# Sliding-window attention with a SwiGLU block: k and q of two chunks transposed by DMA, and the steps around them set in another order

## The chip, the cores and the metric

The kernel runs on one core of one Trainium2 chip. The metric is the device time of one execution in microseconds (us). TensorE is called PE, its weight load PEld, VectorE DVE, ScalarE ACT, GpSimd POOL and SyncE SP, as in the profile. POOL and SP issue most of the DMAs here: POOL the loads from HBM, which also turn float32 into bfloat16, SP the DMA transposes from SBUF to SBUF.

## The reference

Eight batches of eight heads, 576 positions, head dimension 64. Each position attends to itself and the 63 before it; the result, with the heads side by side as 512 features, goes through a SwiGLU block.

```python
scores = scale * np.matmul(q, k.transpose(0, 1, 3, 2))
rel = pos[:, None] - pos[None, :]
mask = (rel >= 0) & (rel < window)          # window = 64
attn = softmax(np.where(mask, scores, -1e9))
x = np.matmul(attn, v)                       # (8, 8, 576, 64) -> (4608, 512)
...
g = x @ w_gate                               # (512, 1536)
silu = g * (1.0 / (1.0 + np.exp(-g)))
val = x @ w_val                              # (512, 1536)
return (silu * val @ w_out).astype(np.float32)   # (1536, 512)
```

## The kernel before, in words

The 4608 rows are cut into 36 **chunks** of 128 rows, n = 0 to 35, and nine **groups** of four chunks (512 rows), c = 0 to 8. A chunk's attention needs its own keys and the 64 before.

What is done to a chunk, by the names in the code:

- *Loading.* `load(n, "kq")` (line 309) brings k and q of one chunk as 128 rows of eight heads of 64, one POOL DMA each (two when a batch ends inside the chunk). `load2(st)` (327) brings k or q of two chunks at once in another layout, eight rows of one head behind each other, 256 KB in one POOL DMA. The rings: eight buffers each of kn and qn, two buffers each for `load2`.
- *Transposing.* The scores need k and q with the head dimension on the partitions, in kT and qT. `T(n, x)` (362) does it with one DMA transpose on SP (recorded at line 370). `T64(st)` (373) does k and q of two chunks from the layout of `load2` with 64 transposes of 64x64 on PE (line 385) into two PSUM banks, from which four copies (line 255 on ACT or 256 on DVE) go to kT and qT.
- *Scores.* `S2(n)` (772) makes the scores of chunks n and n + 1 on PE (24 matmuls each, lines 471 and 475), four exponentials on ACT (483) and two products with the mask on DVE (497).
- *Attention times v.* `B2(n)` (787) is one block: scores of n + 2, the first half of attention times v of n and n + 1 (`AVpair`, line 729), scores of n + 3, the second half, then normalisation on DVE (760, 764) into xb, and the masks.
- *`X(n)`* (799) transposes xb into xT, the input of the feed-forward part; from chunk 6 on by a DMA transpose on SP (808).

And to a group: `F(c, fs, lo, hi)` (926) computes the hidden features fs (blocks of 128, f = 0 to 11) for the rows lo to hi of group c: gate and value matmuls on PE (918), tanh on ACT (899), two products on DVE (904, 906), result in hT. `O(c, u)` and `O2(c, u)` (937, 947) are the output of chunk u of group c, twelve matmuls (962), with the copy out of PSUM on ACT or DVE, and `store` writes it. `F` of half a group with two features is 16 matmuls, and `F` of a whole group with one feature 8.

The order of the work is written out by hand in `build` (1057), call by call up to the second group, then in a loop over the groups from c = 2. The loop begins at line 1195. Each engine has its own queue and takes its instructions in the order of the calls; waits on semaphores are derived from what each step reads and writes. PSUM banks, once `lru` is set, are taken in the order of longest unused. Three things are tied to a place in this order: loads with a gate (`self.lastF`) go out when the F before them has ended on PE, DMA transposes wait in SP's queue in the order of the calls, and POOL's queue likewise.

Around the change the order before is, on PE: AVw(6) and X(6), X(7); T64(4) with its copies on ACT; O(0,1); F(1) of features 6, 7 and 8, 9 on the first half; S2(8); T64(5) with its copies; F(1) of 10, 11 on the first half; F(1) of 0, 1 on the second half; O2(0,2); B2(8); F(1) of 2, 3 and of 4, 5; O2(0,3); B2(10); F(1) of 6, 7, of 8, 9 and of 10, 11; O(1,0), which has F(2) of feature 0 in its middle, behind its ninth matmul; F(2) of feature 1; O2(1,1); B2(12).

Of the kernel before, what the change touches and what calls it, by code (L numbers as in the profile page):

```python
# [153 lines left out]
class _Kernel:  # L154
# [644 lines left out]
    def X(self, n, eng="sp", kind="f"):  # L799
        if n >= NCH:  # L800
            return
        g = self.g
        ix, it, u = n % 4, (n // 4) % self.NX, n % 4
        xb = self.xb[ix]
        xo = self.xT[it][:, :, 128 * u:128 * u + 128]
        xk = [("xb", ix, 0), ("xb", ix, 1)]
        if eng == "sp":
            g.op("sp", lambda e: e.dma_start_transpose(xo, xb[:, :]), reads=xk, writes=[("xT", it, u)], dma=True)
            return
        self.Xp(n, kind)(eng)  # L810
# [115 lines left out]
    def F(self, c, fs, lo=0, hi=512, mid=None, side=False):  # L926
        do = self.Fp(c, fs, lo, hi, side)
        for a in range(len(fs)):
            do("Wg", a)
        if mid:  # L930
            mid()
        do("tan", 0)
        for a in range(len(fs)):
            do("Wv", a)
        do("end", 0)

    def O(self, c, u, mid=None):
        io = (4 * c + u) % self.NO
        self.Omm(c, u, 0, 512, "act", [("ost", io), ("osth", io)], mid=mid)
        self.store(c, u)  # L940
# [95 lines left out]
            self.load(n, "v")  # L1036

    def next_loads(self):
        self.load2(5)

    def after_loads(self):
        for n in (12, 13):
# [14 lines left out]
    def build(self):  # L1057
        F, S, AV, X, O = self.F, self.S, self.AV, self.X, self.O
# [64 lines left out]
        ev = self.T64(2)  # L1123
# [12 lines left out]
        ev = self.T64(3)  # L1136
# [14 lines left out]
        ev = self.T64(4)  # L1151
        for u in range(2):
            ev("k", u, "act")
            ev("q", u, "act")
        O(0, 1)
        F(1, (6, 7), 0, 256)
        self.after_loads()
        F(1, (8, 9), 0, 256)
        self.init_kmask()
        self.S2(8)  # L1160
        ev = self.T64(5)
        for u in range(2):
            ev("k", u, "act")
            ev("q", u, "act")
        for n in (12, 13):
            self.Tkq(n)
        F(1, (10, 11), 0, 256)
        F(1, (0, 1), 256, 512)
        self.O2(0, 2)
# [5 lines left out]
        for n in (14, 15):  # L1175
            self.load(n, "kq", self.lastF)
        F(1, (4, 5), 256, 512)
        self.O2(0, 3)
        self.B2(10)
        self.store(0, 3)  # L1180
        F(1, (6, 7), 256, 512)
        self.T(14, "k")
        X(10)
        X(11)
# [6 lines left out]
        for n in (16, 17, 18):  # L1191
            self.load(n, "kq")
        self.T(16, "q")
        O(1, 0, lambda: F(2, (0,)))
        for c in range(2, NFC):
            for u in range(4):
                n = 4 * c + u + 4
                if (c, u) != (2, 0):
                    F(c, (3 * u,))
                F(c, (3 * u + 1,))  # L1200
                if (c, u) == (3, 0):
                    self.loop_loads(n - 1)
                two = n < NCH and u % 2 == 0
                v = u + 1 if c == 2 else u
                if two:
                    self.O2(c - 1, v)
                elif v < 4 and (n < NCH or u < 3):
                    O(c - 1, v)
                if two:
                    self.B2(n)  # L1210
                    self.store(c - 1, v)
                    if u:
                        X(n)
                        X(n + 1)
                    for m in (n + 4, n + 5):
                        self.T(m, "k")
                    for m in (n + 5, n + 6):
                        self.T(m, "q")
                    if not u:
                        X(n)  # L1220
                        X(n + 1)
                F(c, (3 * u + 2,))
                if u % 2 and n <= NCH and (c, u) != (2, 3):
                    self.loop_loads(n)
                elif (c, u) == (2, 0):
                    for m in (14, 15):
                        self.load(m, "v", self.lastF)
                if n >= NCH and u == 3:
                    O(c - 1, u)
# [46 lines left out]
```

## Time and profile before

| | |
|---|---|
| median of three runs | 325.45 us (325.27 to 325.52) |
| the profiled execution's own time | 325.72 us |
| its span, first to last instruction | 324.0 us |
| PE busy | 314.4 us, 97% |
| DVE, ACT, POOL busy | 218.6, 125.6, 106.5 us |
| PE transposes of line 385 | 256 in the whole kernel, four times 64 |
| DMA transposes of line 370 (k, q) | 48, median 4.0 us to landing |
| DMA transposes of line 808 (xT) | 30, median 3.5 us to landing |

In a timeline row stand the start, the length, the engine, the line, the operation, what is written from what, and the count of merged instructions; behind it in brackets idle time of the engine and what ended it. A row of waits has the engine and line that waited, what it waited for, the total in us, how often, and the longest. A row of DMA issues ends with the median time from issue to landing. Matmuls are pipelined: a row's length holds the tail that the next row overlaps, so the time that work takes on PE is read from start to start.

### The profile page before, as it was taken

To read this page: it belongs to the slowest core of one execution; us is meant where nothing else is said; L and a number is where in the kernel's file an instruction comes from. 1 tells how busy PE (TensorE), PEld (TensorE's weight loads), DVE (VectorE), ACT (ScalarE), POOL (GpSimd) and SP (SyncE) were. 2 spreads that over 40 slices of the span, in tenths; PEclk is the share of its full clock that TensorE was granted. 3 is DMA by queue.
4 is the path that set the end of the run, shared out by engine and by line. 5 is a ranking of instruction groups with operands and counts; after the bars stand their busy time and mean duration, and the time that the engine had idled before them with its cause. 6 is when DMAs were issued, how large, how long until landed. Compare 5 with 4: busy or idle time off the path is not lost.

```text
span 324.0 us, 8018 instructions
## 1 busy us (share of the span) xinstructions
PE 314.4 (97%) x3411; PEld 169.3 (52%) x3446; DVE 218.6 (67%) x408; ACT 125.6 (39%) x226; POOL 106.5 (33%) x138
## 2 busy tenths in 40 slices
PE   7989999999999999999999999999999999999996
PEld 5655677777545454545454544545454544444444
DVE  6778985788576966766767585958586767555510
ACT  3825565643433442433333232424242422222311
POOL 6999711643626061507060607060402000000000
PEclk9999999999999999999999999999999999999999
DMA  7999999999999799959997998999677212000012
GB/s 189 177 197 187 201 184 176 104 169 142 166 155 152 124 109 137 165 103 133 129 120 118 146 139 83 148 133 159 73 110 96 69 34 65 34 32 32 34 65 97
DMA packets 148403, 39.59 MB, mean 122 GB/s; under 512 B 131344, under 2 KB 143376, under 8 KB 148368
## 3 DMA queue, kind: packets, MB, share of 16 engines
q0 software_dynamic: 100032, 18.36, 71.7%
q1 hardware_dynamic: 42864, 10.89, 23.5%
q10 hardware_dynamic: 5472, 9.83, 9.5%
q8 instruction: 27, 0.44, 0.6%
q14 instruction: 8, 0.07, 0.1%
HBM read 37.75 MB, written 9.44 MB: 146 GB/s over the span
## 4 chain that ended last, share of the span: by engine, by line
PE 91%; DMA 2%; POOL 2%; issue 1%; DVE 1%; ACT 1%; ACTq 0%
PE ps L918 56%; PE ps L962 29%; DMA Wv<-in_moe_w_val_dram 2%; PE ps L729 2%; PE ps L521 2%; POOL va L325 1%; PE ps L471 1%; PE ps L475 0%; ACT xT L255 0%; PE ps L385 0%; ACT sig L899 0%; POOL ks L335 0%; PE ps L552 0%; POOL qs L335 0%; POOL Wg L345 0%
## 5 line engine op out<-in xcount | busy, mean ns | idle before, releaser
L918 PE MATMUL ps<-xT,Wv 128*128 128x512 bf16 (+1 forms) x484 | 110.4, 351 | 1.6 <-DMA Wv<-in_moe_w_val_dram 0.9
L904 DVE SCALAR_TENSOR_TENSOR uu<-sig,ps 128x512 bf16<-128x512 bf16 x108 | 73.8, 683 | 56.2 <-ACT sig L899 55.9
L918 PE MATMUL ps<-xT,Wg 128*128 128x512 bf16 (+1 forms) x481 | 107.9, 351 | 2.3 <-issue 2.2
L899 ACT ACTIVATE sig<-ps 128x512 bf16<-128x512 f32 x108 | 64.9, 603 | 89.1 <-PE ps L918 89.1
L962 PE MATMUL ps<-Wo,hT 128*128 128x512 bf16 (+1 forms) x436 | 97.4, 373 | 0.5 <-DVE hT L906 0.2
L906 DVE SCALAR_TENSOR_TENSOR hT<-uu,ps 128x512 bf16<-128x512 bf16 x108 | 74.2, 687 | 4.7 <-PE ps L918 1.0
L918 PEld LDWEIGHTS ps<-xT,Wv 128*128 128x128 bf16 x496 | 48.4, 98 | 45.7 <-DMA Wv<-in_moe_w_val_dram 1.1
L918 PEld LDWEIGHTS ps<-xT,Wg 128*128 128x128 bf16 x496 | 46.8, 98 | 42.7 <-ACT xT L255 0.2
L962 PEld LDWEIGHTS ps<-Wo,hT 128*128 128x128 bf16 x444 | 43.3, 98 | 49.0
L325 POOL DMA_DIRECT2D kn<-in_k_dram x27 | 23.0, 855 | 112.0 <-PE ps L918 112.0
L325 POOL DMA_DIRECT2D va<-in_v_dram x40 | 34.2, 882 | 24.9 <-PE ps L918 24.9
L255 ACT ACTIVATE ost<-ps 128x512 f32<-128x512 f32 (+1 forms) x22 | 12.9, 588 | 53.2 <-PE ps L962 53.2
L531 ACT ACTIVATE pt<-ps 128x512 bf16<-128x512 f32 x36 | 18.6, 602 | 29.0 <-PE ps L521 29.0
L256 DVE COPY ost<-ps 128x512 f32<-128x512 f32 (+1 forms) x15 | 10.1, 673 | 29.2 <-PE ps L962 29.2
L325 POOL DMA_DIRECT2D qn<-in_q_dram x27 | 23.2, 865 | 0.0
L483 ACT ACTIVATE pt<-ps 128x512 bf16<-128x512 f32 x28 | 14.5, 602 | 13.8 <-PE ps L475 13.8
L764 DVE TENSOR_TENSOR xb<-ps,rc 128x512 bf16<-128x512 f32 (+2 forms) x39 | 18.8, 509 | 0.5
L729 PE MATMUL ps<-va,pt 64*64 64x65 bf16 x800 | 12.3, 192 | 0.0
L497 DVE TENSOR_TENSOR pt<-pt,kmask 128x1024 bf16<-128x1024 bf16 x18 | 11.5, 681 | 0.0
L729 PEld LDWEIGHTS ps<-va,pt 64*64 64x64 bf16 x800 | 10.4, 107 | 0.0
L497 DVE TENSOR_TENSOR pt<-pt,mask 128x1024 bf16<-128x1024 bf16 x14 | 9.3, 688 | 1.1 <-ACT pt L483 1.0
L760 DVE RECIPROCAL rc<-ps 128x8 f32<-128x8 f32 (+2 forms) x39 | 5.7, 173 | 6.3 <-PE ps L729 6.3
(76 smaller groups left out, 141.7 us busy)
## 6 DMA issues: line engine op xcount, KB each, us to landing
out_dram<-ost ACTq DMA_DIRECT2D x35, 256.0 KB, 3.3
va<-in_v_dram POOLq DMA_DIRECT2D x32, 128.0 KB, 5.3
kn<-in_k_dram POOLq DMA_DIRECT2D x21, 128.0 KB, 3.9
qn<-in_q_dram POOLq DMA_DIRECT2D x21, 128.0 KB, 4.7
Wg<-in_moe_w_gate_dram POOLq DMA_DIRECT2D x6, 256.0 KB, 7.2
Wv<-in_moe_w_val_dram POOLq DMA_DIRECT2D x6, 256.0 KB, 8.2
Wo<-in_moe_w_out_dram POOLq DMA_DIRECT2D x4, 384.0 KB, 13.6
ks<-in_k_dram POOLq DMA_DIRECT2D x3, 256.0 KB, 10.5
```

What stands on the lines that cost most here:

```text
L255: return self.g.op("act", lambda e: e.activation(d, a, ACTF.Copy), reads=reads, writes=writes, after=after)
L325: self.g.op("pool", lambda e, d=d, a=a: e.dma_start(d, a), writes=ks, dma=True, after=gate)
L483: g.op("act", lambda e, po=po, p=p: e.activation(po, sv[p], ACTF.Exp, scale=SCALE), reads=[bx[p][1]], writes=[pk[p]])
L497: self.g.op("dve", lambda e: e.tensor_tensor(pt, pt, m, ALU.mult), reads=pk + mk, writes=pk)
L531: g.op("act", lambda e, po=po, p=p: e.activation(po, sv[p], ACTF.Exp, scale=SCALE), reads=[bx[p][1]], writes=[pk[p]])
L729: x = e.matmul(o, ab[0], ab[1], start=first, stop=phase == 1, skip_group_check=True)
L764: g.op("dve", lambda e, av=av, hs=hs, w=w, rc=rc, xo=xo: e.tensor_tensor(xo[:, :, hs, :], av[:, :, :, 0:64], rc[:, :, hs].unsqueeze(3).to_ ...
L899: g.op("act", lambda e: e.activation(sig[:, 0:w], G[:, 0:w], ACTF.Tanh, scale=0.5), reads=[gk], writes=[("sig", i)])
L904: g.op("dve", lambda e: e.scalar_tensor_tensor(uu[:, 0:w], sig[:, 0:w], 1.0, G[:, 0:w], ALU.add, ALU.mult), reads=[("sig", i), gk], writes ...
L906: g.op("dve", lambda e: e.scalar_tensor_tensor(out, v3(uu), 0.5, v3(V), ALU.mult, ALU.mult), reads=[("uu", i), vk], writes=[("hT", ih, f, ...
L918: r = e.matmul(bank[:, a * n:a * n + n], W[:, kk, f * 128:f * 128 + 128], xT[:, kk, lo:hi], start=(kk == 0), stop=(kk == NK - 1))
L962: r = e.matmul(OB[:, 0:n], hT[:, f, 128 * u:128 * u + 128], self.Wo[:, f, lo:hi], start=(f == 0), stop=(f == NF - 1))
```

## The change

Chunks 10 and 11 no longer go through `load2` and T64(5): k and q of each are loaded singly (four POOL DMAs) and transposed by four DMA transposes on SP, which stand in SP's queue behind X(7) and ahead of those of chunks 12 and 13. S2(8) moves up by two F steps, behind O(0,1), and the F of 6, 7, 8, 9 follow it, so that the gate of the loads of 12, 13 (the F of 6, 7) lies behind S2(8). F(1) of 6, 7 on the second half goes ahead of O2(0,3) and B2(10). O(1,0) is no longer split; O(1,1) follows it, and then F(2) of feature 0. In the loop's first group O2(1,2) takes the place of O2(1,1), O2(1,3) stays, and O(1,2) is gone from between them; O(1,1) is copied out by ACT in place of DVE, O(1,2) by DVE in place of ACT.

```diff
     def next_loads(self):
-        self.load2(5)
+        for n in (10, 11):
+            self.load(n, "kq")
...
         O(0, 1)
+        self.init_kmask()
+        self.S2(8)
+        for n in (10, 11):
+            self.Tkq(n)
         F(1, (6, 7), 0, 256)
         self.after_loads()
-        F(1, (8, 9), 0, 256)
-        self.init_kmask()
-        self.S2(8)
-        ev = self.T64(5)
-        for u in range(2):
-            ev("k", u, "act")
-            ev("q", u, "act")
         for n in (12, 13):
             self.Tkq(n)
+        F(1, (8, 9), 0, 256)
         F(1, (10, 11), 0, 256)
...
         F(1, (4, 5), 256, 512)
+        F(1, (6, 7), 256, 512)
         self.O2(0, 3)
         self.B2(10)
         self.store(0, 3)
-        F(1, (6, 7), 256, 512)
...
-        O(1, 0, lambda: F(2, (0,)))
+        O(1, 0)
+        O(1, 1)
+        F(2, (0,))
...
-                v = u + 1 if c == 2 else u
+                v = (2, 4, 3, 4)[u] if c == 2 else u
```

## The prediction

> **What bounds the kernel now.** I read the page first: engine shares, clock, the chain that ended last. The list of what TensorE (PE) waited for came next, over 49 to 324 us, all that follows the edits.
>
> ```profile
> span 324.0 us, 8018 instructions
> PE 314.4 (97%) x3411; PEld 169.3 (52%) x3446; DVE 218.6 (67%) x408; ACT 125.6 (39%) x226; POOL 106.5 (33%) x138
> PEclk9999999999999999999999999999999999999999
> PE 91%; DMA 2%; POOL 2%; issue 1%; DVE 1%; ACT 1%; ACTq 0%
> PE ps L918 <- issue: 1.9, 12, 0.2
> PE ps L962 <- DVE hT L906: 0.2, 1, 0.2
> ```
>
> PE is busy for 97% of the span at the full granted clock and makes 91% of the chain. The last two rows are its whole list of waits after 49 us: 1.9 us of issue in 12 places, and 0.2 us once. So from 49 us PE is a solid row of work: PE work taken out moves the end by its own length, and any wait of PE put in moves it back by the length of the wait. No other engine is near being the bound.
>
> **The change part by part.**
>
> *The transposes of 10, 11 leave PE.* T64(5) is 64 small transposes between S2(8) and F. The neatest price is a pair of places with the same 48 score matmuls: S2(6) followed by F directly, S2(8) with T64(5) in between.
>
> ```profile
> 42.52 0.24 PE L471 MATMUL ps<-qT,kT 64*64 64x128 bf16 x2
> 43.15 1.05 PE L918 MATMUL ps<-xT,Wg 128*128 128x256 bf16 x8
> ...
> 56.80 0.24 PE L471 MATMUL ps<-qT,kT 64*64 64x128 bf16 x2
> ...
> 57.29 0.22 PE L385 MATMUL ps<-ident,ks 64*64 64x64 bf16 x2
> ...
> 57.56 0.47 PE L385 MATMUL ps<-ident,qs 64*64 64x64 bf16 x32
> 57.96 1.05 PE L918 MATMUL ps<-xT,Wg 128*128 128x256 bf16 x8
> ```
>
> Scores to next F: 43.15 - 42.52 = 0.63 us without, 57.96 - 56.80 = 1.16 us with. The difference, **0.53 us**, is what T64(5) costs PE. Its bounds: not below zero, since the matmuls are gone for certain; and not over 0.67 us, from its first start at 57.29 to F at 57.96. All of it lies on the path. The four copies of its result on ACT go too; ACT is busy for 39% of the span and not on the path here, so that gives nothing.
>
> *S2(8) directly behind O(0,1).* It needs k, q of 8, 9, copied out of T64(4) on ACT.
>
> ```profile
> 52.19 0.62 ACT L255 ACTIVATE qT<-ps 128x512 bf16<-128x512 bf16 x1
> 53.21 0.27 PE L918 MATMUL ps<-xT,Wg 128*128 128x256 bf16 x1
> ```
>
> The last copy ends at 52.19 + 0.62 = 52.81. O(0,1) ends where F starts now, 53.21, and S2(8) cannot begin before that: 0.4 us in hand, and more for chunk 9, which is second. Cost nothing; if the copies slipped by one of their own lengths, 0.62, it would be 0.2. On ACT four exponentials now stand ahead of F(6,7)'s tanh. PE doesn't wait for a tanh as such, only for a PSUM bank, and it takes the bank of eight that was left alone longest: the F groups behind S2(8) get those of T64(4), of O(0,1) and, from the third on, of S2(8), which the exponentials have left by then, since two groups take 3.5 us. Cost nothing; without that cover it would be a part of one exponential.
>
> *Loads of 10, 11.* Two 256 KB loads become four of 128 KB.
>
> ```profile
> 37.10 1.78 POOL L325 DMA_DIRECT2D va<-in_v_dram  x2
> 40.95 0.70 POOL L335 DMA_DIRECT2D ks<-in_k_dram  x1 [2.06 <-PE ps L385]
> 55.42 0.88 POOL L325 DMA_DIRECT2D kn<-in_k_dram  x1 [12.97 <-PE ps L918]
> qs<-in_q_dram POOLq DMA_DIRECT2D x1, 256.0 KB, 12.5
> ```
>
> POOL pays 4 x 0.87 instead of 2 x 0.7, but no longer waits 2.06 us for PE to free the row buffers, since the k and q buffers 2 and 3 have not been used. So it issues from 38.88 to 42.4, where it then stands idle for 12.97 us: free. With the slowest landing here, 12.5 us, the last is in by 41.5 + 12.5 = 54.0. If smaller pieces cost 3 us more, that is 57, still ahead of its reader's turn (58.35, next). The loads of 12, 13 wait for F(6,7), which moves behind S2(8): 0.7 us later (its 0.63 and a small step ahead of it), so 56.1 in place of 55.42.
>
> *Four DMA transposes on SP.* This is the cost that before does not show.
>
> ```profile
> 51.64 2.76 SPq L808 DMA_TRANSPOSE xT<-xb  x2
> 58.96 1.19 SPq L370 DMA_TRANSPOSE kT<-kn  x1
> 140.05 2.52 SPq L370 DMA_TRANSPOSE kT<-kn  x2
> 142.61 2.57 SPq L370 DMA_TRANSPOSE qT<-qn  x2
> 64.15 0.24 PE L471 MATMUL ps<-qT,kT 64*64 64x128 bf16 x2
> 64.67 0.24 PE L471 MATMUL ps<-qT,kT 64*64 64x128 bf16 x1
> ```
>
> SP is done with X(6), X(7) at 54.40 and then idle until 58.96. A transpose takes it 1.28 us ((142.61 - 140.05) / 2), 1.30 with the step between. The four go out at 54.45, 55.75, 57.05 and **58.35**, and SP is free at 59.6, when k of 12 comes in (58.96 + 0.7): the transposes behind move by 0.7 us for the gate, not for the queue. The readers are in B2(8): scores of 10 at 64.15 - 0.53 = 63.62, scores of 11 at 64.67 - 0.53 = 64.14. So the last transpose, q of 11, may take 5.79 us from issue to landing. What they take in this trace, minimum, median, maximum:
>
> ```profile
> DMA to landing us min/median/max: 2.5/2.5/2.6
> DMA to landing us min/median/max: 4.4/4.9/5.1
> DMA to landing us min/median/max: 6.8/7.0/7.2
> DMA to landing us min/median/max: 6.1/7.0/7.8
> 115.93 0.88 POOL L325 DMA_DIRECT2D kn<-in_k_dram  x1 [12.50 <-PE ps L918]
> 119.33 1.25 SPq L370 DMA_TRANSPOSE kT<-kn  x1
> ```
>
> The first row is 109 to 115 us, no loads about; the second 62 to 66, beside the tail of the loads of 12, 13, the very loads that ours meets; the third and fourth 119 to 122 and 217 to 219, issued 3.4 us (119.33 - 115.93) and more after a burst of loads began. Ours goes out 58.35 - 56.1 = 2.2 us into its burst. Bounds 2.5 and 7.8; I take **5.1**, the upper end of the row with the same loads: landing 63.45, 0.7 ahead of need, cost nothing. The margin is thin; both ends go into the range.
>
> The Trainium skill, "VectorE: DVE Perf Modes", section "The three transpose paths", prices a 128x128 bf16 transpose at 390 ns on TensorE against 1309 ns by DMA, and its rules prefer TensorE: it speaks against this change. By its figure the sixteen such blocks of 10, 11 would free 6.2 us of PE (an estimate); the trace says 0.53 for all, and the trace decides. Its order of latencies agrees, 2.5 us at best on the DMA.
>
> *Block 10 a step later.* F(6,7) of the second half goes ahead of O2(0,3) and B2(10): the same PE work in another order.
>
> ```profile
> 59.72 1.04 PE L918 MATMUL ps<-xT,Wg 128*128 128x256 bf16 x8
> 71.63 0.24 PE L471 MATMUL ps<-qT,kT 64*64 64x128 bf16 x2
> 64.93 1.19 SPq L370 DMA_TRANSPOSE qT<-qn  x1
> ```
>
> One F of two groups takes 59.72 - 57.96 = 1.76. B2(10) begins at 71.63 + 1.76 - 0.53 = 72.86, its second scores some 0.5 later, 73.4. The last transpose of 13 goes out at 64.93 + 0.7 = 65.6; even 7.2 us put it at 72.8, in time. Without this move the need would be 71.6 and that case late: the move pays for the delayed loads. SP's later entries (k of 14, X(10), X(11)) keep their order behind it.
>
> *Second output of group 1 ahead of group 2.* F(2,0) reads what X(10), X(11) bring, now 1.23 us later (72.86 - 71.63).
>
> ```profile
> 74.02 2.50 SPq L808 DMA_TRANSPOSE xT<-xb  x2
> xT<-xb SPq DMA_TRANSPOSE x2, 4.4
> 80.05 1.03 PE L918 MATMUL ps<-xT,Wg 128*128 128x512 bf16 x4
> 81.78 0.81 PE L962 MATMUL ps<-Wo,hT 128*128 128x512 bf16 x3
> 84.15 2.75 PE L962 MATMUL ps<-Wo,hT 128*128 128x512 bf16 x12
> 86.83 0.24 PE L471 MATMUL ps<-qT,kT 64*64 64x128 bf16 x2
> 93.75 2.57 SPq L808 DMA_TRANSPOSE xT<-xb  x2
> ```
>
> X(11), issued near 74.02 + 1.25 = 75.27, lands by about 75.27 + 4.4 + 1.23 = 80.9. In the old order F(2,0) would start at 80.05 - 0.53 = 79.5 and wait 1.4 us. Behind the last three matmuls of O(1,0) (0.6, their 0.81 less the tail that the next covers) and all of O(1,1) (2.6 likewise) it starts at 82.7: 1.8 us in hand. O(1,1) and O(1,2) read only what group 1 has finished, into output buffers stored long before. B2(12) comes 2.6 - 0.53 = 2.1 us later, at 88.9, with SP's turn for X(12) at 93.75 still behind it; B2(14) is where it was, less 0.53.
>
> **Sum.** -0.53 against the profiled execution's own 325.72 us (span 324.0 and 1.72 around it): 325.19. That execution stands 0.27 above the median of the runs shown, 325.45; from the median the forecast is **324.92**.
>
> **The rivals.**
>
> *The last transpose is late and the kernel slower.* A mix of loads and transposes is what gave 7.0. Then q of 11 lands at 65.35 and PE stands 1.21 us at the scores of 11: 325.45 - 0.53 + 1.21 = 326.13; with 7.8, 326.93. The wait starts above 5.79, eats the gain at 6.32, and at 6.97 the kernel is slower by 0.65. For it: ours is inside a burst, with three transposes just ahead in the same queue. Against: its burst is only 2.2 us old, and the same loads gave 5.1 at most. The Trainium skill, "DMA: Bandwidth & Descriptors", section "Issuing engines are not separate DMA queues", says that DMAs of all issuers share the same 16 engines and interleave; by that rule this wait can come although SP itself is free, and 2.5 against 7.0 in this trace agrees.
>
> *A part wait.* Landing 5.8 to 6.9 us after issue: a wait of 0 to 1.1, so 324.9 to 326.0, middle 325.4: no change to see.
>
> *More goes than T64(5).* With T64(5) at its upper bound and the one 0.2 us wait on hT (the second row of the waits) gone as well, 325.45 - 0.67 - 0.2 = 324.58.
>
> **How the numbers follow.** Forecast 0.57, part wait 0.26, late and slower 0.11, more gone 0.06. Measurement here tells about 0.2%, 0.65 us, from no change; the forecast's 0.53 lies inside. A spread of 0.15 in the medians puts about a quarter of the forecast's chance past 0.65. Faster by over 0.2%: 0.14 + 0.06 = 0.20; slower: 0.11 and 0.02 of the part wait, 0.13; within: 0.67. The range is 324.5 to 326.0: it takes in the larger gain and the part wait and leaves out the late transposes.
>
> **What would show it.** No L385 rows near 57 us, and F 0.63 us behind S2(8)'s first scores; B2(8) at 63.6 with its second scores 0.52 behind. If those gaps grow, the list of waits will name PE L471 or L475 waiting for a DMA into qT or kT: the late rival. S2(8) starting past 53.4 would make the ACT copies the fault, F(2,0) waiting for a DMA into xT the moved block. Wrong altogether would be an end that moves while those places stand as forecast.

## The result, and the profile after

The changed kernel takes 327.55 us (median of 22 runs, 324.92 to 331.01); the kernel before took 325.35 beside it (22 runs, 324.96 to 326.86). The ratio is 1.0059, 95% interval 1.0039 to 1.0080: slower by 0.6%, where 0.53 us less was forecast, and beyond the upper end of the range, 326.0. It is also more spread out. The spread has an order: in ten of the 22 runs the mean granted TensorE clock is 0.994 or 0.995, and their median is 328.6; in eleven it is 0.999 or 1.000, and their median is 326.25. (One run, 331.01 at 0.989, is left out of the ratio.) Of the 91 runs of the kernel before that stand beside the experiments below, one has a clock under 0.999.

The profiled execution is one of the eleven, 325.87 us. The page's first lines:

```profile
span 324.1 us, 7930 instructions
PE 317.1 (98%) x3382; PEld 168.7 (52%) x3382; DVE 218.6 (67%) x408; ACT 123.9 (38%) x222; POOL 108.7 (34%) x140
PEclk9999999999999999999999999999999999999999
```

64 PE transposes have gone, four ACT copies too, and the span is as long as it was. The list of what PE waited for, over the same 49 to 324 us as in the prediction, has two rows that were not there:

```profile
PE ps L471 <- DVE ost L256: 0.4, 1, 0.4
PE ps L918 <- issue: 0.3, 1, 0.3
```

The 1.9 us of issue in 12 places that stood in the prediction's list are gone, but they were no time. The page of before has 3411 matmul records beside 3446 weight loads, this one 3382 beside 3382; every trace of this case with that row lacks 35 or 36 matmul records, and every trace without it lacks none. The 0.2 us at line 962 in the prediction's list is a missing record too: the twelve matmuls of O(0,1) stand there as eleven. The busy time of PE, up from 314.4 to 317.1, says no more: two profiles of one and the same kernel further down have 317.0 without the row and 314.2 with it.

The timeline of PE shows the two places (rows left out between them):

```profile
52.87 0.24 PE L471 MATMUL ps<-qT,kT 64*64 64x128 bf16 x2
...
53.51 0.28 PE L918 MATMUL ps<-xT,Wg 128*128 128x256 bf16 x1
...
57.88 1.04 PE L918 MATMUL ps<-xT,Wv 128*128 128x256 bf16 x8
59.22 1.03 PE L918 MATMUL ps<-xT,Wg 128*128 128x256 bf16 x8 [0.30 <-issue]
...
63.65 0.24 PE L471 MATMUL ps<-qT,kT 64*64 64x128 bf16 x2
...
64.82 0.24 PE L471 MATMUL ps<-qT,kT 64*64 64x128 bf16 x2 [0.45 <-DVE ost L256]
...
65.48 1.05 PE L918 MATMUL ps<-xT,Wg 128*128 128x256 bf16 x8
...
67.24 1.04 PE L918 MATMUL ps<-xT,Wg 128*128 128x256 bf16 x8
```

S2(8) to F is 53.51 - 52.87 = 0.64 us: T64(5) is gone, as forecast. But F(0,1) of the second half starts 59.22 - 57.88 = 1.34 after the row before it, where two such rows take 1.76 (67.24 - 65.48), so one 0.88: 0.46 lost. And B2(8), from its first scores to the next F, takes 65.48 - 63.65 = 1.83. Before, its first scores stood at 64.15 (a row of the prediction) and the next F at 65.44, so it took 1.29:

```profile
65.44 0.39 PE L918 MATMUL ps<-xT,Wg 128*128 128x256 bf16 x2
```

That is 0.54 lost, ahead of the scores of chunk 11. The sum closes: S2(8) stands at 52.87, where F stood at 53.21 before (a row of the prediction), so all starts 0.34 earlier, and -0.34 - 0.53 + 0.46 + 0.54 = +0.13 us, where the spans differ by 0.1. The start is scatter: the kernel with the late moves alone, below, is the kernel before up to this place and has F there at 52.81.

What had both waited for? The transposes that they read, by the issues on SP:

```profile
52.55 1.75 SPq L808 DMA_TRANSPOSE xT<-xb  x1
54.35 1.26 SPq L370 DMA_TRANSPOSE kT<-kn  x1
55.66 1.26 SPq L370 DMA_TRANSPOSE qT<-qn  x1
56.97 1.66 SPq L370 DMA_TRANSPOSE kT<-kn  x1
58.67 1.27 SPq L370 DMA_TRANSPOSE qT<-qn  x1
```

and their times to landing, the two of line 808 around 52 us (X(6), X(7)), and the two of line 370 from 56.97 on (k and q of 11):

```profile
DMA to landing us min/median/max: 4.6/5.6/6.6
```

```profile
DMA to landing us min/median/max: 5.7/5.9/6.1
```

X(7), issued at 52.55, lands 6.6 us later at 59.13, and F starts at 59.22. q of 11, issued at 58.67, lands 6.1 later at 64.73, and its scores start at 64.82. Both start 0.09 us behind the landing. So the names in the list of waits mislead twice: "issue" and "DVE ost" stand for a DMA whose semaphore came last. The DVE copy that was named ended at 64.44, 0.38 before the scores; and before the change the same scores stood at 64.67 (a row of the prediction), in the middle of the same copy. The copy after, and before:

```profile
63.75 0.69 DVE L256 COPY ost<-ps 128x512 f32<-128x512 f32 x1 [1.42 <-PE ps L962]
```

```profile
64.47 0.68 DVE L256 COPY ost<-ps 128x512 f32<-128x512 f32 x1
```

Before, X(6) and X(7) landed after

```profile
DMA to landing us min/median/max: 3.3/3.4/3.5
```

### The profile page after: what moved, and what is told of

It is laid out like the page before. It is cut to its first block, busy times and chain, and to the rows that moved or that the text cites. A ratio compares the mean times of both kernels' runs of the same rounds, so it can differ in the third digit from the quotient of the medians.

```text
span 324.1 us, 7930 instructions
## 1 busy us (share of the span) xinstructions
PE 317.1 (98%) x3382; PEld 168.7 (52%) x3382; DVE 218.6 (67%) x408; ACT 123.9 (38%) x222; POOL 108.7 (34%) x140
## 4 chain that ended last, share of the span: by engine, by line
PE 92%; POOL 2%; DMA 1%; DVE 1%; ACT 1%; issue 1%; ACTq 0%; POOLq 0%
PE ps L918 57%; PE ps L962 29%; PE ps L729 2%; PE ps L521 2%; DMA hT<-in_q_dram 1%; PE ps L471 1%; POOL vs L256 1%; ACT pt L483 1%; POOL va L325 1%; DVE ost L256 1%; POOL Wv L345 0%; POOL Wg L345 0%; DVE uu L904 0%; PE ps L385 0%; PE ps L475 0%
## 5 line engine op out<-in xcount | busy, mean ns | idle before, releaser
L918 PE MATMUL ps<-xT,Wg 128*128 128x512 bf16 (+1 forms) x496 | 111.2, 352 | 0.4 <-issue 0.3
L325 POOL DMA_DIRECT2D kn<-in_k_dram x29 | 24.8, 858 | 109.5 <-PE ps L918 109.5
L325 POOL DMA_DIRECT2D qn<-in_q_dram x29 | 25.0, 867 | 0.0
```

What stands on the lines that cost most here:

```text
L325: self.g.op("pool", lambda e, d=d, a=a: e.dma_start(d, a), writes=ks, dma=True, after=gate)
L918: r = e.matmul(bank[:, a * n:a * n + n], W[:, kk, f * 128:f * 128 + 128], xT[:, kk, lo:hi], start=(kk == 0), stop=(kk == NK - 1))
```

## The experiments

Theory A: PE waits for DMA transposes that land too late in the crowd of loads and transposes between 52 and 66 us. Rival B: the moves cost, S2(8) upward or the late part. Rival C: it is the clock or the start of the kernel, not the waits. Times are medians; the kernel before was run beside each.

**The changed kernel once more**, unedited, to see what the executions at 0.995 hold.

> The changed kernel once more, for a second profile and more times. Theory A (late DMAs): the transposes of 10, 11 crowd the DMA engines with X(7) and the loads of 12, 13; PE waits at F(0,1) of the second half for X(7) and at the scores of 11 for q of 11, 0.46 and 0.54 us in the first profile, and by other amounts from execution to execution: median 327 to 328, spread over 324.9 to 330, and in a longer execution these two waits (or the like for 12, 13) are longer by what the time is longer. Theory B (the moved steps cost): the same median, but the time is lost at S2(8), O(1,1) or B2(10), and these two waits stay at 0.5.

326.86 us (326.37 to 328.70, six runs) against 325.43, ratio 1.0062 (1.0041 to 1.0082). The profiled execution took 328.36, with a mean clock of 0.995. The list of PE's waits after 49 us has one row; in the second row the first time is that of q of 10 and the last that of q of 11; the timeline has the place:

```profile
PE ps L471 <- DMA qT<-qn: 1.8, 1, 1.8
```

```profile
DMA to landing us min/median/max: 6.5/6.8/7.1
```

```profile
52.80 0.24 PE L471 MATMUL ps<-qT,kT 64*64 64x128 bf16 x2
...
63.12 0.24 PE L471 MATMUL ps<-qT,kT 64*64 64x128 bf16 x2
...
65.69 0.24 PE L471 MATMUL ps<-qT,kT 64*64 64x128 bf16 x2 [1.84 <-DMA qT<-qn]
...
66.42 1.89 PE L918 MATMUL ps<-xT,Wg 128*128 128x256 bf16 x8
68.11 1.78 PE L918 MATMUL ps<-xT,Wv 128*128 128x256 bf16 x8
69.72 1.04 PE L918 MATMUL ps<-xT,Wg 128*128 128x256 bf16 x8
```

Here X(7) was in time, so B2(8) began at 63.12 and needed q of 11 sooner; it took 7.1 us and PE waited 1.84. Then something new: two F rows take 69.72 - 66.42 = 3.30 us where the trace above has 67.24 - 65.48 = 1.76 for the same two. That is 1.54 us more, on work that waits for nothing. The windows give the reason; behind the busy times of the five engines stand the granted clock, the DMA engines' share and the GB/s:

```profile
66.00:66.25 0.25, 0.25 (x46) 0.25 (x32) 0.00 (x0) 0.08 (x1) 0.00 (x0) 0.90 2.49 157
66.25:69.50 3.25, 3.25 (x32) 2.26 (x19) 2.98 (x9) 1.61 (x3) 0.00 (x0) 0.50 1.52 186
69.50:69.75 0.25, 0.25 (x4) 0.17 (x3) 0.25 (x2) 0.00 (x0) 0.00 (x0) 0.78 0.09 13
```

The clock is 0.50 for 3.4 us, 3.25 in the middle row and 0.05 and 0.11 in the rows at its edges: 0.50 x 3.4 = 1.7 us lost. Of these 1.54 fall on the two rows, and 0.1 on the end of B2(8). So a wait of 1.84 us cost 3.5. Over the whole run that is a mean clock of 1 - 1.7 / 326 = 0.995, as ten of the first 22 runs have it (0.994 or 0.995). Theory A had the place right, but gave 327 to 328 and laid a longer execution to longer waits alone; half of what this wait cost is the clock behind it.

**Only the DMA transposes, in the old order.** Chunks 10, 11 by DMA, T64(5) gone, nothing moved.

```diff
-        self.load2(5)
+        for n in (10, 11):
+            self.load(n, "kq")
...
         O(0, 1)
+        for n in (10, 11):
+            self.Tkq(n)
         F(1, (6, 7), 0, 256)
...
-        ev = self.T64(5)
-        for u in range(2):
-            ev("k", u, "act")
-            ev("q", u, "act")
```

> Before's order with k, q of 10, 11 by DMA alone: four single loads, four transposes on SP behind X(7), T64(5) gone, nothing else moved. Theory A: as slow and as spread as the changed kernel or more so, 327 to 330, since B2(10) has no longer 1.76 us of room for the transposes of 12, 13 either. Theory B: 0.53 us faster than before, 324.9.

328.98 us (328.73 to 329.05, four runs), ratio 1.0111 (1.0098 to 1.0124): the slowest of all. Waits, landing of k and q of 11, and the window behind:

```profile
PE ps L471 <- DMA qT<-qn: 2.7, 1, 2.7
```

```profile
DMA to landing us min/median/max: 7.7/7.9/8.1
```

```profile
67.50:70.75 3.25, 3.25 (x18) 2.23 (x16) 3.24 (x8) 1.04 (x2) 0.17 (x1) 0.50 1.48 223
```

The quarter of a microsecond at either end of this window has 0.85 and 0.82, so the half clock lasts 3.4 us here too and costs 1.7; it begins 1.1 us after the wait has ended, in the repeated run 0.5. All four runs have a mean clock of 0.994 or 0.995.

The swap alone makes the loss, and more of it: the old order sends the loads of 12, 13 out at 54.77 in place of 55.72, into the same crowd. For A. The moves in the change soften this.

**All moves, but T64(5) kept**, with `load2(5)`, at its new place behind S2(8). Against the changed kernel:

```diff
     def next_loads(self):
-        for n in (10, 11):
-            self.load(n, "kq")
+        self.load2(5)
...
         self.S2(8)
-        for n in (10, 11):
-            self.Tkq(n)
+        ev = self.T64(5)
+        for u in range(2):
+            ev("k", u, "act")
+            ev("q", u, "act")
         F(1, (6, 7), 0, 256)
```

> All moves of the change, but k, q of 10, 11 still by the 256 KB loads and T64(5) on PE, which stands behind S2(8) in its new place. Theory A: no transposes by DMA are added, so 325.3, within 0.3 us of the kernel before and as narrow in its spread. Theory B: 327 or more, as the changed kernel.

326.96 us (326.49 to 327.44, five runs), ratio 1.0052 (1.0040 to 1.0064): a miss for A, which wanted no change. Two more kernels split it. **The late moves alone** (block of 10 a step later, O(1,1) ahead of group 2) in the order of before:

```diff
+        F(1, (6, 7), 256, 512)
         self.O2(0, 3)
         self.B2(10)
         self.store(0, 3)
-        F(1, (6, 7), 256, 512)
...
-        O(1, 0, lambda: F(2, (0,)))
+        O(1, 0)
+        O(1, 1)
+        F(2, (0,))
...
-                v = u + 1 if c == 2 else u
+                v = (2, 4, 3, 4)[u] if c == 2 else u
```

> The kernel before with the two later moves alone: B2(10) a step later, O(1,1) ahead of group 2; T64(5) and S2(8) where they were. If these moves cost nothing: 325.4. If they are what made the moves-only kernel slow (1.0 us of issue at F(8,9) of the second half, right behind B2(10)): 326.4, with that wait in the trace.

325.55 us against 325.48, ratio 1.0003 (0.9992 to 1.0014), and PE's waits after 49 us are the two rows of before, unchanged. They cost nothing. **S2(8) and T64(5) up, nothing else:**

```diff
         O(0, 1)
+        self.init_kmask()
+        self.S2(8)
+        ev = self.T64(5)
+        for u in range(2):
+            ev("k", u, "act")
+            ev("q", u, "act")
         F(1, (6, 7), 0, 256)
         self.after_loads()
+        for n in (12, 13):
+            self.Tkq(n)
         F(1, (8, 9), 0, 256)
-        self.init_kmask()
-        self.S2(8)
-        ev = self.T64(5)
-        for u in range(2):
-            ev("k", u, "act")
-            ev("q", u, "act")
-        for n in (12, 13):
-            self.Tkq(n)
```

> The kernel before, with S2(8) and T64(5) behind O(0,1) and ahead of F(6,7) and F(8,9), and the loads of 12, 13 behind F(6,7), as in the changed kernel; load2(5), T64(5) and all later moves as before. Of the kernel with all moves and T64(5) kept (1.5 us slower than before) it holds one half; the other half, the late moves, cost nothing. Theory A (the order around T64(5) costs: 0.37 us behind the copies of T64(5) and the wait for its row buffers): 325.8 to 327.0, and its profile has a wait of PE L385 and nothing new near 75 us. Theory B (the 0.9 us of issue near 75 us is an accident of the whole order, as to where PE's instructions and a standstill of the DMA engines meet, and makes most of the 1.5): within 0.4 us of before, 325.3 to 325.8.

326.52 us against 325.30, ratio 1.0034 (1.0021 to 1.0047). Two rows of its timeline of PE carry idle time:

```profile
53.92 0.45 PE L385 MATMUL ps<-ident,ks 64*64 64x64 bf16 x32 [0.21 <-DMA qs<-in_q_dram]
...
76.49 0.71 PE L918 MATMUL ps<-xT,Wg 128*128 128x256 bf16 x5 [1.09 <-issue]
```

The first belongs to T64(5), which now stands too early for the landing of its own load; the changed kernel has no T64(5) and no such wait. The second falls in the middle of an F, as in the kernel with all moves, at 75.98 there, 0.86. The time is theory A's, but a row near 75 us is what only theory B had, so neither holds whole. Neither profile of the changed kernel has this second stop, nor have the two of the next kernel; whether executions without a profile have it is not known. What PE waited for there stays open, as the trace has no semaphore event at that matmul.

**Both readers later.** The changed kernel with O2(0,2) ahead of F(0,1) of the second half, so that X(7) has 2.6 us more, and with F(2,3) of the second half ahead of B2(8), so that q of 11 has 1.76 more. All PE work stays, and so do all DMAs.

```diff
         F(1, (10, 11), 0, 256)
-        F(1, (0, 1), 256, 512)
         self.O2(0, 2)
+        F(1, (0, 1), 256, 512)
+        F(1, (2, 3), 256, 512)
         self.B2(8)
         self.store(0, 2)
         X(8)
         X(9)
-        F(1, (2, 3), 256, 512)
```

> The changed kernel with both readers of the late DMAs moved back: O2(0,2) ahead of F(0,1) of the second half (2.6 us more for X(7)), and F(2,3) of the second half ahead of B2(8) (1.76 us more for k, q of 11). The same PE work. Theory A: the waits go in most executions, 324.8 to 325.3, 0.3 to 0.5 us faster than before, narrow again. Theory B: 327 to 328, as the changed kernel.

324.79 us (324.49 to 326.60, twelve runs), ratio 0.9988 (0.9973 to 1.0002): 0.64 below before. PE has no row of waits at all after 49 us, while the transposes are as slow as ever (q of 10, q of 11 and k of 11, in the order of their times):

```profile
DMA to landing us min/median/max: 5.0/5.9/6.6
```

q of 11, issued at 59.55, lands 5.9 us later at 65.45, and its scores start only at 65.87. The same transposes, just as late, and the loss is gone: A, and B falls for all moves that this kernel keeps. The same kernel once more:

> The changed kernel with both readers later, once more: its first median was 0.64 us below before, with an interval that just touches no change. Theory (PE saves the 0.53 us of T64(5) and waits for no transpose): 324.6 to 325.1 and a ratio of 0.9975 to 0.9990, its interval below 1. Rival (the first was luck; the transposes are late in part of the executions here too): median 325.3 or more, ratio 1.000 or more.

325.17 us against 325.60, ratio 0.9986 (0.9972 to 1.0000), again 0.43 below, though a little over the 325.1 forecast, and with an interval that again just touches no change. The two differences, 0.64 and 0.43, lie around the 0.53 that T64(5) was priced at. No run of its 24 has a clock under 0.999, so the low clock goes with the waits, and rival C falls as a cause of its own.

**One reader at a time.** Only O2(0,2) ahead of F(0,1):

```diff
-        F(1, (0, 1), 256, 512)
         self.O2(0, 2)
+        F(1, (0, 1), 256, 512)
         self.B2(8)
```

> The changed kernel with O2(0,2) ahead of F(0,1) of the second half alone: 2.6 us more for X(7), nothing more for k, q of 11. If the wait for q of 11 in B2(8) is the main loss: 326.3 to 327, at most 0.5 us less than the changed kernel, and the wait in the trace 0.5 to 2.5 us. If X(7) is: 325.0.

325.87 us against 325.48, ratio 1.0014 (1.0004 to 1.0024). Only F(2,3) ahead of B2(8):

```diff
         self.O2(0, 2)
+        F(1, (2, 3), 256, 512)
         self.B2(8)
...
-        F(1, (2, 3), 256, 512)
```

> The changed kernel with F(2,3) of the second half ahead of B2(8) alone: 1.76 us more for k, q of 11, nothing more for X(7). If q of 11 is the main loss: 324.9 to 325.4, and the wait in B2(8) 0 to 0.9 us. If X(7) is: 326.5 to 327.

325.57 us against 325.48, ratio 1.0005 (0.9994 to 1.0016). Each alone takes most of the loss away, and neither gives the 0.53 us back; the first lies between its two forecasts, and the second, 0.2 above its own, still has a wait of 0.2 at the scores of 11 in its profile. Of the first, the wait and two windows:

```profile
PE ps L471 <- DMA qT<-qn: 1.6, 1, 1.6
```

```profile
63.00:66.50 3.50, 1.94 (x119) 1.75 (x119) 1.66 (x4) 1.84 (x4) 0.00 (x0) 1.00 2.31 150
66.50:70.00 3.50, 3.50 (x35) 3.13 (x33) 3.47 (x9) 1.53 (x3) 1.86 (x3) 1.00 1.17 178
```

Nothing held PE ahead of B2(8) here, and q of 11 is waited for in full, 1.6 us, much as in the repeated run; but the clock stays at 1.00, and the execution takes 326.41 and not 328.36. All eleven runs of this kernel have a clock of 0.999 or more. Why it holds in this order, in which F and not O2 stands ahead of the gap, is not settled. So the stretch of half clock is a term of its own: there behind 1.84 and 2.7 us, not behind 1.6.

**The loads of 12, 13 behind F(8,9)**, 1.75 us later, readers as in the change:

```diff
         F(1, (6, 7), 0, 256)
+        F(1, (8, 9), 0, 256)
         self.after_loads()
         for n in (12, 13):
             self.Tkq(n)
-        F(1, (8, 9), 0, 256)
```

> The changed kernel with the loads of 12, 13 (and v of 10, 11) gated by the F of 8, 9 in place of the F of 6, 7: 1.75 us later. If it is these loads that hold up the transposes of 11: q of 11 lands 3 to 5 us after its issue instead of 6 to 7, no wait in B2(8), 324.9 to 325.3 (unless k, q of 13 are then late for B2(10)). If the transposes hold up each other in SP's queue and behind the loads of 10, 11: 6 to 7 us as before, 326.9.

325.94 us (324.63 to 326.95, ten runs), ratio 1.0011 (0.9996 to 1.0027). Landing of q of 10, k of 11 and q of 11, in this order, and the wait left:

```profile
DMA to landing us min/median/max: 2.5/4.1/5.8
```

```profile
PE ps L471 <- DVE ost L256: 0.3, 1, 0.3
```

The time lies between the two forecasts, and one of the ten runs has a clock of 0.995. q of 10 lands after 2.5 us here, and after 3.8 in the next kernel, which holds the same loads back; in the six profiles of the changed order with the loads in their place it took 5.0 to 6.5. q of 11 goes out at 58.90, 0.9 us behind the first of these loads even here, and its 5.8 is no less than the 5.2 and 5.9 of the kernel with both readers later. The loads are a part of the crowd, not all of it.

**Both together**, readers later and loads later, was to be the best:

> The changed kernel with both readers later (O2(0,2) ahead of F(0,1) of the second half, F(2,3) of the second half ahead of B2(8)) and with F(8,9) ahead of the loads of 12, 13. Theory (the late transposes of X(7) and of q of 11 are all that the change loses): no wait of PE for them is left and more is in hand, so 324.4 to 324.9, about 0.6 below before, with fewer executions above 326 than with both readers later alone. Rival (something else in the changed order costs, clock or fetch): 325.2 or more, or as many executions above 326.

It was not: 326.88 us (325.37 to 329.50, twelve runs) against 325.30, ratio 1.0050 (1.0027 to 1.0073). Waits, the place in the timeline, and the landing of k and q of 13, issued at 66.04 and 67.34:

```profile
PE ps L471 <- issue: 2.3, 1, 2.3
```

```profile
75.73 0.24 PE L471 MATMUL ps<-qT,kT 64*64 64x128 bf16 x2 [2.29 <-issue]
```

```profile
DMA to landing us min/median/max: 6.5/7.4/8.3
```

The issue on SP, and the window of PE behind the wait:

```profile
67.34 2.49 SPq L370 DMA_TRANSPOSE qT<-qn  x1
```

```profile
76.40:80.00 3.60, 3.60 (x36) 3.24 (x34) 3.49 (x9) 2.10 (x4) 0.00 (x0) 1.00 0.44 115
```

q of 13 went out at 67.34 and landed 8.3 later, at 75.64; its scores in B2(10) start at 75.73. The wait is of the same kind, a block later: holding back the loads had held back the transposes behind them. q of 13 now went out 1.9 us behind the first of the loads of 14, 15 (65.46); in the second profile with both readers later it went out at 65.31, 0.3 ahead of them, and landed after 5.2. And though it is longer than the 1.84 above, the clock behind it stays at 1.00; two of the twelve runs have 0.995.

## Why the prediction was wrong

- *T64(5) is worth 0.53 us:* right. S2(8) to F is 0.64 us after, against 0.63 forecast, and the kernel with both readers later is 0.64 and 0.43 below before. (The 0.2 us of a wait on hT that the rival "more goes" added was a missing record.)
- *S2(8) behind O(0,1), block 10 later, the second output ahead of group 2:* right at nothing for each, as far as the changed kernel shows. No PE row waits at any of these places after; the late two were tried alone (1.0003).
- *The last transpose, q of 11, takes 5.1 us:* this is the step that failed. It took 6.1, 6.7, 7.1 and 8.1 us in the four profiles with its reader and the loads in place, and 5.2 to 8.1 in all nine with these transposes, always above 5.1; in hand were 5.79. It was issued at 58.67, 0.3 later than forecast, since the third transpose held SP 1.66 us in place of 1.28. The value was taken from the upper end of a row beside the tail of the same loads. The row of 7.0, transposes inside a burst, was the right one: the new transposes meet the loads of 12, 13, and with X(6), X(7) they are six in a row. That the loads are a part of it is shown by the kernel with the loads later; what the rest is made of stays open. The rule of the Trainium skill named in the prediction ("DMA: Bandwidth & Descriptors", section "Issuing engines are not separate DMA queues") held: SP was free, and the wait came all the same.
- *X(6), X(7), and the loads of 10, 11 as free:* free on POOL, and in time for their own readers, but what their tail does to X(6), X(7) was not priced at all. X(7) took 6.6 us in place of 3.5 and held F(0,1) for 0.46 in one profile. The rows are packets, MB and time of packets of the loads' queue, the time as a share of the 16 engines' (packets overlap, so it can pass 100%); before and after from 50 to 52 us, then before and after from 52 to 54:

```profile
q0 software_dynamic: 382, 0.33, 102.9%
q0 software_dynamic: 2359, 0.30, 233.4%
q0 software_dynamic: 26, 0.02, 6.3%
q0 software_dynamic: 878, 0.11, 86.2%
```

  From 50 to 52 us the loads now move the same bytes in six times as many packets, and their tail reaches to where X(6) and X(7) are issued, 51.21 and 52.55. The four transposes follow from 54.35 on. In the kernel with the moves and T64(5), X(6) and X(7) have neither beside them:

```profile
DMA to landing us min/median/max: 3.0/3.2/3.3
```

  No run has the one without the other, so how much each of them takes is not shown. In the other profiles of the changed order X(7) took 4.3 to 5.0 and nobody waited, but for the last experiment, where it took 6.6 as well, though the loads of 12, 13 go out there only at 57.63, 4.9 us after it; so these loads are not what held it:

```profile
DMA to landing us min/median/max: 4.5/5.5/6.6
```

```profile
57.63 0.88 POOL L325 DMA_DIRECT2D kn<-in_k_dram  x1 [15.31 <-PE ps L918]
```

- *The rival "late and slower", 0.11:* the right mechanism at the right place, with too small a chance and too small a price. It counted the wait at its length, 1.21 to 2.0 us. The wait measured 0.5 to 2.7, and behind two of them, of 1.84 and 2.7, PE then ran 3.4 us at half its clock, 1.7 us more; no term of the prediction stands for that. In the repeated run the sum from the profile of before is -0.41 (S2(8) at 52.80 in place of 53.21) - 0.53 + 2.0 (B2(8) 3.30 in place of 1.29) + 1.54 = +2.6, and the spans, 326.6 and 324.0, differ by 2.6. The range ended with the part wait and left this rival out; its own highest figure, 326.93 for a landing of 7.8, was too low as well, where a landing of 7.1 made 328.36.

The Trainium skill, "TensorE: Matmul & The Clock Gate", Part 1, says that PE's clock has two levels, full and half, and falls to half after an idle window of about 3.4 us. The depth and the length agree (0.50 over 3.4 us, in both traces). The length of gap that it asks for does not: 1.84 and 2.7 us of idle time were enough here, while 1.6 and 2.29 were not. The measurement decides. The same section says that the window runs freely; that a gap's place in it decides would fit 1.84 with and 2.29 without, but no run here was made to show it.

## What to carry to other kernels

Where PE is full, moving PE work to the DMA engines gains only that work's length, and puts the landing time of the transfer into the path: price the landing from a row with the same mix of loads and transposes, at its upper end, for every transfer in the crowd, also those already there. A wait of PE of about 2 us may cost nearly twice its length, since a stretch of half clock can follow. What mended it was to move the readers behind other PE work and not the transfers: that left a gain of 0.43 and 0.64 us here, at the edge of what can be told from none, while holding back the loads besides moved the wait to the next block.

## What the runs showed of the hardware

- A DMA transpose of one chunk lands after 2.5 us when it is alone (before, 109 to 115 us), and among loads and other transposes q of 11 landed after 5.2 to 8.1 and q of 13 once after 8.3; X(7), issued in the tail of the loads of 10, 11 and ahead of the four new ones, went from 3.5 to 6.6 in two of the profiles.
- One gap of PE of 1.84 us (and of 2.7) was followed by 3.4 us at a granted clock of 0.50; gaps of 1.6 and 2.29 were not. Length alone does not decide.
- Where several semaphores are waited for, the list of waits named "issue" (0.3 and 2.3 us) or a DVE copy (0.4 and 0.3) for what the landing times show to be DMA transposes.
